# A listed order of work units, stores held back until the last load, and a narrower transpose stride in an attention and token-mixing kernel

## The chip, the cores and the metric

The kernel runs on one core of one Trainium2 chip. The metric is the device time of one execution in microseconds (us). A time is given as a median with the lowest and highest run. Runs more than 1.5% above the fastest run of the same kernel are counted as slow and take no part in ratios.

Engines are named as in the profile: PE is the tensor engine, PEld its weight loads, DVE the vector engine, ACT the scalar engine, POOL GpSimd, SP the sync engine that issues the stores.

## The reference

```python
# q, k, v: (8 batches, 8 heads, 576, 64) f32;  w_q, w_k: (512, 64);  w_out: (512, 512)
scores = scale * q_c @ k_c.T             # within chunks of 64 positions
attn   = softmax(scores)
x      = (attn @ v_c) as (8, 576, 512)   # heads side by side
wq, wk = x @ w_q, x @ w_k
W_tok  = scale * wq @ wk.T               # 576 x 576 for each batch
out    = relu(W_tok @ x) @ w_out         # (8, 576, 512) f32
```

## The kernel before

All of q, k and v is loaded by GpSimd, cast to f16 on the way, with one tile for each batch and part, so no load waits for a buffer. A batch is cut into units. T transposes q or k on DVE, in part 0 (5 row groups) or part 1 (4 row groups). S makes a quarter of the scores and their exponential. A multiplies them with v and divides. X transposes x on PE. K, Q and G are the small products of the mixing layer, M mixes, and O makes one of the 36 output tiles and stores it. Before the change a short list for one cycle is repeated, each unit with the lag that its inputs force, and four PSUM slots (places in the memory that matmuls write to) are taken in rotation:

```python
ORDER = "A3 M3 X0 O1 X1 Tk0 O1 K Tq0 Tq1 Q G S1 S0 O1 Tk1 M0 O1 O1 A0 S3 S2 A1 M1 M2 A2"

def pair(fill=0):                       # the next PSUM slot, in rotation
    turn[0] += 1
    a = ring[turn[0] % 4]
    for _ in range(fill):               # two 128x512 matmuls of zeros per unit of S, A, X in batch 0
        nc.tensor.matmul(a[:, 0, :], lhsT=zero[:, 0:P], rhs=zero[:], start=True, stop=True)
    return a

def tr(b, which):                       # q and k alike: f32 pairs written at stride 4 (16 bytes)
    nc.vector.transpose(out=dst[b % 2].bitcast(F32)[...].rearrange("p (t w r) -> p t r w", r=R, w=32), in_=...)

def outp():
    # ... four matmuls ...
    os_ = osb[n % NOSB]                 # five buffers
    nc.scalar.copy(os_[:], a[:, 0, :])
    nc.sync.dma_start(of[n * P : n * P + P, :], os_[:])   # the store goes at once
```

The loads are issued in this order: q and k of batch 0, its v, the weights, then batch after batch (cuts are marked by `...`).

The softmax here doesn't subtract the row's maximum and nothing guards it: scores larger than these inputs give would overflow.

Of the kernel before, what the change touches and what calls it, by code (L numbers as in the profile page):

```python
# [10 lines left out]
F16 = mybir.dt.float16  # L11
F32 = mybir.dt.float32
# [4 lines left out]
ORDER = """  # L17
A3 M3 X0 O1 X1 Tk0 O1 K Tq0 Tq1 Q G S1 S0 O1 Tk1 M0 O1 O1 A0 S3 S2 A1 M1 M2 A2
""".split()

NEEDS = {
    "S0": ("Tq0", "Tk0"),
    "S1": ("Tq0", "Tk0"),
    "S2": ("Tq1", "Tk1"),
    "S3": ("Tq1", "Tk1"),
    "A0": ("S0", "S1"),
    "A1": ("S0", "S1"),
    "A2": ("S0", "S1", "S2", "S3"),
    "A3": ("S2", "S3"),
    "X0": ("A0", "A1"),  # L30
    "X1": ("A2", "A3"),
    "Q": ("X0", "X1"),
    "K": ("X0", "X1"),
    "G": ("K", "X0", "X1"),
    "M0": ("Q", "G"),
    "M1": ("M0",),
    "M2": ("M1",),
    "M3": ("M2",),
}


def lags(order):
    at = {u: n for n, u in enumerate(order)}
    lag = {}

    def of(u):
        if u not in lag:
            lag[u] = max(
                [of(d) + (1 if at[d] > at[u] else 0) for d in NEEDS.get(u, ())] + [0]
            )  # L50
        return lag[u]

    for u in order:
        if u[0] != "O":
            of(u)
    return lag
# [3 lines left out]
def kernel(  # L60
# [32 lines left out]
    def each(n, shape, dt, name):  # L93
        return [sb.tile(shape, dt, name=f"{name}{i}") for i in range(n)]
# [21 lines left out]
    NOSB = 5  # L116
    osb = each(NOSB, [P, DM], F32, "osb")
# [15 lines left out]
    def load_v(b):  # L133
        nc.gpsimd.dma_start(  # L134
            vt[b][:, :, 0:D], vf[b].rearrange("(t p) d -> p t d", p=P)
        )

    nc.vector.memset(zero[:], 0.0)  # L138
    load_qk(0, 0)
    load_qk(0, 1)  # L140
    load_v(0)
    make_identity(nc, ident[:])
    nc.gpsimd.dma_start(wqd[:, :, 0:DH], moe_w_q.rearrange("(i p) j -> p i j", p=P))
    nc.gpsimd.dma_start(wk[:], moe_w_k.rearrange("(i p) j -> p i j", p=P))
    nc.gpsimd.dma_start(wout[:], moe_w_out.rearrange("(i p) m -> p i m", p=P))
    for b in range(1, B):
        load_qk(b, 0)
        load_v(b)
        load_qk(b, 1)
# [7 lines left out]
    turn = [0]  # L157

    def pair(fill=0):
        turn[0] += 1  # L160
        a = ring[turn[0] % 4]
        for _ in range(fill):
            nc.tensor.matmul(a[:, 0, :], lhsT=zero[:, 0:P], rhs=zero[:], start=True, stop=True)  # L163
        return a

    def tr(b, which):
        part = int(which[1])
        a, e = TR[part]
        src, dst = (qn, qT) if which[0] == "q" else (kn, kT)
        nc.vector.transpose(  # L170
            out=dst[b % 2]
            .bitcast(F32)[:, 2 * CH * a : 2 * CH * e]
            .rearrange("p (t w r) -> p t r w", r=R, w=32),
            in_=src[b][part].bitcast(F32).rearrange("p t (r d) -> p t r d", d=32),
        )

    def operand(buf, b, t, i, ch, e):
        o = t * R * D + ch * P
        return buf[b % 2][32 * i : 32 * i + 32, o : o + P].rearrange(
            "p (c e) -> p c e", e=2  # L180
        )[:, :, e]

    def scores(b, s, fill):
        rows, part = s % 2, s // 2
        t0, t1 = TR[part]
        a = pair(fill)
        for t in range(t0, t1):
            for e in range(2):
                for ch in range(2):
                    for i in range(2):  # L190
                        nc.tensor.matmul(  # L191
                            a[CH * ch : CH * ch + CH, i, (t - t0) * CH : (t - t0) * CH + CH],
                            lhsT=operand(kT, b, t, 2 * rows + i, ch, e),
                            rhs=operand(qT, b, t, 2 * rows + i, ch, e),
# [11 lines left out]
    def attend(b, kk, fill):  # L206
        a = pair(fill)
# [34 lines left out]
    def xtr(b, n, fill):  # L242
        a = pair(fill)
# [10 lines left out]
    def mlp_q(b):  # L254
        if b == 0:
            nc.vector.tensor_copy(wqd[:, :, DH:], wqd[:, :, 0:DH])  # L256
        a = pair()
# [11 lines left out]
    def mlp_k(b):  # L269
        a = pair()  # L270
# [13 lines left out]
    def mlp_g(b):  # L284
        a = pair()
# [11 lines left out]
    done = {"out": 0, "ready": 0}  # L297

    def mix(b, n):
        i, half = n % 2, n // 2  # L300
        a = pair()
# [15 lines left out]
        if i == 1:  # L317
            done["ready"] = ((2 * b + half + 1) * HS) // P

    def outp():  # L320
        n = done["out"]
        if n >= done["ready"]:
            return
        done["out"] = n + 1
        a = pair()
# [9 lines left out]
        os_ = osb[n % NOSB]  # L335
        nc.scalar.copy(os_[:], a[:, 0, :])  # L336
        nc.sync.dma_start(of[n * P : n * P + P, :], os_[:])

    lag = lags(ORDER)
    FILL = 2  # L340
    for _ in range(2):
        pair(7)
    for cycle in range(B + max(lag.values())):
        for u in ORDER:
            if u[0] == "O":
                outp()
                continue
            b = cycle - lag[u]
            if not 0 <= b < B:
                continue  # L350
            fill = FILL if b == 0 else 0
            if u[0] == "T":
                tr(b, u[1:])
            elif u[0] == "S":
                scores(b, int(u[1]), fill)
            elif u[0] == "A":
                attend(b, int(u[1]), fill)
            elif u[0] == "X":
                xtr(b, int(u[1]), fill)
            elif u == "Q":  # L360
                mlp_q(b)
            elif u == "K":
                mlp_k(b)
            elif u == "G":
                mlp_g(b)
            else:
                mix(b, int(u[1]))
    while done["out"] < done["ready"]:
        outp()
# [30 lines left out]
```

## Time and profile before

| | |
|---|---|
| time | 148.67 us median of the 3 runs (148.11 to 151.46) |
| span of the profiled execution | 149.3 us (one of the longer runs) |
| last load packet | 97.3 us |
| last matmul of the work | 145.4 us |
| data moved | 14.81 MB of loads as landed, 9.44 MB of stores |

The page, the batch windows and the four stalls are shown and read in the prediction below. First, windows cut where PE goes on past instructions 960 and 3008. Both numbers are 192 more than a multiple of 256, like those of the four stalls that the prediction shows in this trace (960, 1728, 2240 and 2752), each of which ended 2.3 to 2.5 us after the start of a packet of 16384 bytes on the queue that the page calls "instruction". The 256 instructions from one such place to the next are called a block here, and the place a boundary. The columns are: window, its length, then each engine's busy us with its instruction count, the granted clock of PE, DMA share, and GB/s.

```profile
core 0: us, PE busy (x) PEld busy (x) DVE busy (x) ACT busy (x) POOL busy (x), PEclk, DMA share, GB/s
0.00:39.85 39.85, 24.97 (x479) 12.74 (x479) 16.92 (x34) 7.33 (x11) 26.10 (x32) 0.76 1.61 165
39.85:96.99 57.14, 47.94 (x1023) 30.12 (x1024) 35.82 (x54) 27.84 (x48) 17.29 (x18) 0.81 1.70 210
96.99:149.30 52.31, 44.45 (x1001) 26.59 (x998) 30.79 (x46) 33.37 (x58) 0.00 (x0) 1.00 0.30 115
```

The middle row is eight blocks of 256 PE instructions (a matmul and a weight load count as two), 57.14 us. The q transposes among the groups of DVE: the last figure before the second bar is the mean length of one in ns.

```profile
L170 DVE STREAM_TRANSPOSE qT<-qn 128x640 f32<-128x640 f32 x8 | 10.4, 1295 | 0.0
...
L170 DVE STREAM_TRANSPOSE qT<-qn 128x512 f32<-128x512 f32 x8 | 8.6, 1072 | 0.0
```

### The profile page before, as it was taken

What the parts mean: (1) busy time and instruction counts of PE and PEld (TensorE: products, weight loads), DVE (VectorE), ACT (ScalarE), POOL (GpSimd) and SP (SyncE); (2) the same over time, 40 slices, a digit from 0 to 9 for tenths busy, and PEclk for the clock granted to TensorE, in tenths of its full rate; (3) what the DMA queues carried; (4) which work ended last, traced back from release to release, by engine and by line L of the source; (5) the groups of instructions that cost most, each with busy time, mean ns of one, the idle gap of its engine ahead of it and who ended that gap; (6) DMA issues with size and microseconds to landing.
All of it is one profiled execution on the core that took longest, in us unless ns stands there. A gap on an engine that the chain in (4) does not pass through costs nothing. (4 is left out here: it accounts for less than half of the span.)

```text
span 149.3 us, 5506 instructions
## 1 busy us (share of the span) xinstructions
PE 117.4 (79%) x2498; PEld 69.4 (47%) x2498; DVE 83.5 (56%) x133; ACT 68.5 (46%) x117; POOL 43.4 (29%) x49
## 2 busy tenths in 40 slices
PE   6626998176399881999689839989898798989890
PEld 2212436145166461564457426564574565566330
DVE  2082256932197764484577627493996799393000
ACT  3002200017143881139533836158748846864871
POOL 7996671662824612732730000000000000000000
PEclk9995557968659998579969995699999999999999
DMA  1999999999999999999999999921330312413254
GB/s 11 175 178 161 202 177 177 196 164 190 189 168 195 251 166 261 190 195 228 228 245 175 259 191 228 180 101 74 146 137 8 145 70 75 158 61 141 114 199 179
DMA packets 62725, 24.58 MB, mean 165 GB/s; under 512 B 39152, under 2 KB 58096, under 8 KB 62704
## 3 DMA queue, kind: packets, MB, share of 16 engines
q0 software_dynamic: 57520, 14.81, 100.5%
q1 hardware_dynamic: 5184, 9.44, 17.4%
q8 instruction: 19, 0.31, 0.8%
q14 instruction: 2, 0.02, 0.0%
HBM read 29.62 MB, written 9.44 MB: 262 GB/s over the span
## 5 line engine op out<-in xcount | busy, mean ns | idle before, releaser
L328 PE MATMUL ring<-wout,rmx 128*128 128x512 f16 x144 | 40.6, 416 | 0.4 <-ACT osb L336 0.2
L336 ACT COPY osb<-ring 128x512 f32<-128x512 f32 x36 | 21.1, 586 | 26.5 <-PE ring L328 25.8
L199 ACT ACTIVATE est<-ring 128x640 f16<-128x640 f32 (+1 forms) x32 | 19.6, 648 | 24.3 <-PE ring L191 23.9
L233 DVE TENSOR_TENSOR xn<-ring,rec 128x640 f16<-128x640 f32 x32 | 26.4, 824 | 1.1
L232 DVE RECIPROCAL rec<-ring 128x10 f32<-128x10 f32 x32 | 6.9, 217 | 32.7 <-PE ring L223 27.0
L191 PE MATMUL ring<-qT,kT 32*64 32x64 f16 x1152 | 14.7, 202 | 12.2 <-issue 5.8
L170 DVE STREAM_TRANSPOSE kT<-kn 128x640 f32<-128x640 f32 (+1 forms) x16 | 19.3, 1205 | 5.8 <-DMA kn<-in_k_dram 5.8
L311 ACT ACTIVATE rmx<-ring 128x576 f16<-128x576 f32 x32 | 19.8, 653 | 3.5 <-PE ring L303 3.1
L191 PEld LDWEIGHTS <-kT 32*64 32x64 f16 x1152 | 12.3, 111 | 17.8 <-issue 9.2
L328 PEld LDWEIGHTS <-rmx 128*128 128x128 f16 x144 | 13.5, 106 | 14.1 <-issue 3.6
L252 DVE COPY xt<-ring 128x1280 f16<-128x1280 f16 x16 | 13.2, 822 | 11.0 <-PE ring L247 10.7
L128 POOL DMA_DIRECT2D qn<-in_q_dram x16 | 13.1, 817 | 18.6 <-DMA vt<-in_v_dram 17.8
L247 PE MATMUL ring<-ident,xn 128*128 128x128 f16 x160 | 15.5, 258 | 3.5 <-issue 3.1
L170 DVE STREAM_TRANSPOSE qT<-qn 128x640 f32<-128x640 f32 (+1 forms) x16 | 17.7, 1184 | 0.0
L247 PEld LDWEIGHTS <-xn 128*128 128x128 f16 x160 | 13.1, 118 | 8.5 <-issue 6.8
L128 POOL DMA_DIRECT2D kn<-in_k_dram x16 | 13.0, 810 | 11.3 <-DMA kn<-in_k_dram 6.7
L134 POOL DMA_DIRECT2D vt<-in_v_dram x8 | 14.8, 1847 | 5.0 <-DMA kn<-in_k_dram 3.5
L223 PE MATMUL ring<-vt,est 64*64 64x65 f16 x576 | 12.4, 211 | 4.0 <-DVE xn L233 1.7
L223 PEld LDWEIGHTS <-est 64*64 64x64 f16 x576 | 9.1, 119 | 13.0 <-issue 9.9
L267 ACT CAST wqT<-ring 128x576 f16<-128x576 f32 x8 | 5.1, 638 | 21.7 <-PE ring L260 21.7
L163 PE MATMUL ring<-zero 128*128 128x512 f16 x34 | 13.9, 544 | 1.2 <-DVE zero L138 1.2
L260 PE MATMUL ring<-xt,wqd 128*128 128x288 f16 x64 | 9.9, 300 | 3.7 <-DVE wqd L256 3.7
(28 smaller groups left out, 69.8 us busy)
## 6 DMA issues: line engine op xcount, KB each, us to landing
out_dram<-osb SPq DMA_DIRECT2D x36, 256.0 KB, 2.5
vt<-in_v_dram POOLq DMA_DIRECT2D x8, 576.0 KB, 18.0
qn<-in_q_dram POOLq DMA_DIRECT2D x8, 320.0 KB, 14.2
kn<-in_k_dram POOLq DMA_DIRECT2D x8, 320.0 KB, 15.5
qn<-in_q_dram POOLq DMA_DIRECT2D x8, 256.0 KB, 17.6
kn<-in_k_dram POOLq DMA_DIRECT2D x8, 256.0 KB, 17.5
wout<-in_moe_w_out_dram POOLq DMA_DIRECT2D x1, 512.0 KB, 10.3
wqd<-in_moe_w_q_dram POOLq DMA_DIRECT2D x1, 64.0 KB, 8.0
```

Source lines behind the costliest of these rows:

```text
L128: nc.gpsimd.dma_start(dst[b][part][:], src[b].rearrange("(t p r) d -> p t (r d)", p=P, r=R)[:, a:e, :],)
L134: nc.gpsimd.dma_start(vt[b][:, :, 0:D], vf[b].rearrange("(t p) d -> p t d", p=P))
L163: nc.tensor.matmul(a[:, 0, :], lhsT=zero[:, 0:P], rhs=zero[:], start=True, stop=True)
L170: nc.vector.transpose(out=dst[b % 2] .bitcast(F32)[:, 2 * CH * a : 2 * CH * e] .rearrange("p (t w r) -> p t r w", r=R, w=32), in_=src[b][p ...
L191: nc.tensor.matmul(a[CH * ch : CH * ch + CH, i, (t - t0) * CH : (t - t0) * CH + CH], lhsT=operand(kT, b, t, 2 * rows + i, ch, e), rhs=oper ...
L199: nc.scalar.activation(est[b % 2][s].rearrange("p i t c -> p i (t c)")[:, :, 0:n], a[:, :, 0:n], AF.Exp, scale=scale_attn,)
L223: nc.tensor.matmul(a[CH * (c % 2) : CH * (c % 2) + CH, hh, jj * W : jj * W + D + 1], lhsT=lhsT, rhs=rhs, start=True, stop=True,)
L233: nc.vector.tensor_tensor(out=xn[b % 2][:, :, 2 * kk * D : 2 * kk * D + 2 * D].rearrange("p j (i d) -> p i j d", i=2), in0=xv[:, :, :, 0:D ...
L247: nc.tensor.transpose(tx[:, i, j * P : j * P + P], xn[b % 2][:, j, (2 * n + i) * P : (2 * n + i) * P + P], ident[:],)
L311: nc.scalar.activation(rmx[(b // 2) % 2].rearrange("p (h i) n -> p i h n", h=2)[:, i, :, o : o + HS], a[:, :, 0:HS], AF.Relu, scale=scale_moe,
L328: nc.tensor.matmul(a[:, 0, :], lhsT=rmx[pr % 2][:, i, tl * P : tl * P + P], rhs=wout[:, i, :], start=(i == 0), stop=(i == NI - 1),)
L336: nc.scalar.copy(os_[:], a[:, 0, :])
```

## The change

The change gives every unit its place by hand and takes the stores away from the loads. The whole program is one list of units with the PSUM slot after the colon (S31:0 is quarter 3 of the scores of batch 1, in slot 0). The idle fill matmuls are nearly gone. v of batch 0 comes in two halves, the first ahead of part 1 of q and k. The second half of wqd is loaded, not copied on DVE. q is transposed to stride 8 bytes, and the score matmuls read it accordingly. Each of the first 32 outputs lies in the q or k tile of a batch that is no longer needed, so no output waits for a buffer. A small copy out of the last loaded k tile stands ahead of the first store on the same queue, so that no store starts before the last load has landed (in the trace after, the last load packet ended at 88.3 us, and the sync engine issued the copy at 88.91 and the first store at 89.75); this copy is called the gate below. The diff is shortened: edits are left out without a mark, among them the function by which the score matmuls read q.

```diff
-ORDER = """ A3 M3 X0 O1 X1 Tk0 O1 K Tq0 Tq1 Q G S1 S0 O1 Tk1 M0 O1 O1 A0 S3 S2 A1 M1 M2 A2 """
+PLAN = """
+Tq00 Tk00 Tq10 S10:0 S00:1 Tk10 A00:2 S20:3 S30:0 A10:1 F:2 A20:2 A30:3 X00:0 X10:1 Tk01
+Tq01 Q0:2 K0:3 S11:0 S01:1 G0:2 A01:3 Tq11 M00:0 Tk11 A11:1 Tq02 M10:2 M20:0 Tk02 M30:3
+O:2 S31:0 S21:3 O:2 O:1 A21:0 A31:3 O:2 X01:1 S02:0 S12:2 X11:3 A02:0 K1:1 Tq12 Tk12
+... (ten more lines)
+"""
     load_qk(0, 0)
+    load_v(0, 0, NV // 2)
     load_qk(0, 1)
-    load_v(0)
+    load_v(0, NV // 2, NV)
-    nc.gpsimd.dma_start(wqd[:, :, 0:DH], moe_w_q.rearrange("(i p) j -> p i j", p=P))
+    nc.gpsimd.dma_start(wqd[:, :, 0:DH], wqv)
+    nc.gpsimd.dma_start(wqd[:, :, DH:], wqv)
+        if which[0] == "q":
+            o = o.rearrange("p (u w l) -> p u l w", l=2, w=32)
+        else:
+            o = o.rearrange("p (t w r) -> p t r w", r=R, w=32)
-        os_ = osb[n % NOSB]
-        nc.scalar.copy(os_[:], a[:, 0, :])
-        nc.sync.dma_start(of[n * P : n * P + P, :], os_[:])
+        if n < 4 * B:
+            home = (qn, kn)[n % 2][n // 4][(n // 2) % 2]
+            os_ = home.rearrange("p t c -> p (t c)").bitcast(F32)[:, 0:DM]
+        else:
+            os_ = spare[n - 4 * B][:]
+        nc.scalar.copy(os_, a[:, 0, :])
+        if n == GATE:                                    # GATE = 0
+            nc.sync.dma_start(mark[:], kn[B - 1][1][0:1, 0, 0:2])
+        nc.sync.dma_start(of[n * P : n * P + P, :], os_)
-    FILL = 2
... (the lags, the rotation and the per-unit fills are removed)
```

More of the change, by code (lines that the diff above doesn't have):

```diff
@@ L15 @@
 PSUM = bass.MemoryType.PSUM
-ORDER = """
-A3 M3 X0 O1 X1 Tk0 O1 K Tq0 Tq1 Q G S1 S0 O1 Tk1 M0 O1 O1 A0 S3 S2 A1 M1 M2 A2
-""".split()
-NEEDS = {
-    "S0": ("Tq0", "Tk0"),
-    "S1": ("Tq0", "Tk0"),
-    "S2": ("Tq1", "Tk1"),
-    "S3": ("Tq1", "Tk1"),
-    "A0": ("S0", "S1"),
-    "A1": ("S0", "S1"),
-    "A2": ("S0", "S1", "S2", "S3"),
-    "A3": ("S2", "S3"),
-    "X0": ("A0", "A1"),
-    "X1": ("A2", "A3"),
-    "Q": ("X0", "X1"),
-    "K": ("X0", "X1"),
-    "G": ("K", "X0", "X1"),
-    "M0": ("Q", "G"),
-    "M1": ("M0",),
-    "M2": ("M1",),
-    "M3": ("M2",),
-}
-def lags(order):
-    at = {u: n for n, u in enumerate(order)}
-    lag = {}
-    def of(u):
-        if u not in lag:
-            lag[u] = max(
-                [of(d) + (1 if at[d] > at[u] else 0) for d in NEEDS.get(u, ())] + [0]
-            )
-        return lag[u]
-    for u in order:
-        if u[0] != "O":
-            of(u)
-    return lag
+PLAN = """
+Tq00 Tk00 Tq10 S10:0 S00:1 Tk10 A00:2 S20:3 S30:0 A10:1 F:2 A20:2 A30:3 X00:0 X10:1 Tk01
+Tq01 Q0:2 K0:3 S11:0 S01:1 G0:2 A01:3 Tq11 M00:0 Tk11 A11:1 Tq02 M10:2 M20:0 Tk02 M30:3
+O:2 S31:0 S21:3 O:2 O:1 A21:0 A31:3 O:2 X01:1 S02:0 S12:2 X11:3 A02:0 K1:1 Tq12 Tk12
+Q1:2 G1:3 A12:0 Tq03 M01:1 M11:2 S22:3 Tk03 S32:1 X02:0 M21:2 O:3 S13:1 A22:2 S03:0
+A32:3 O:1 A03:2 M31:0 X12:3 Tq13 Tk13 A13:1 O:0 O:2 K2:3 Q2:0 S33:2 S23:1 Tq04 Tk04 G2:3
+O:0 A23:2 M02:1 M12:3 X03:0 A33:1 S04:2 S14:3 Tq14 O:0 X13:2 A04:1 M22:3 Tk14 O:0 Q3:2
+K3:3 M32:1 A14:0 S24:2 Tk05 S34:3 G3:1 O:0 A24:2 M03:3 Tq05 O:1 M13:0 A34:3 X04:2 S05:1
+S15:0 Tq15 X14:3 O:1 Tk15 O:2 K4:0 M23:3 A05:1 S25:2 Tq06 S35:0 G4:3 A15:1 M33:2 Q4:0
+A25:3 A35:2 X05:1 O:0 O:3 M04:2 M14:0 Tk06 O:1 X15:3 S06:2 S16:0 O:1 Tk16 Tq16 K5:3
+M24:2 A06:0 S36:1 S26:3 O:2 G5:0 M34:1 Tk07 A16:3 A26:2 Q5:0 Tq07 O:1 M05:3 A36:0 Tq17
+O:2 M15:1 Tk17 S17:3 S07:0 X16:2 X06:1 O:3 M25:2 A07:0 S27:1 K6:3 A17:2 S37:0 G6:1 M35:3
+A27:0 A37:2 Q6:1 O:3 M06:0 M16:1 X17:2 X07:3 O:0 O:2 K7:1 Q7:3 M26:0 M36:2 G7:1 O:3 O:0
+M07:2 M17:1 O:3 O:0 O:2 M27:1 M37:3 O:0 O:2 O:1 O:3 O:0
+"""
 @with_exitstack
@@ L115 @@
     rmx = each(2, [P, NI, 2 * S], F16, "rmx")
-    NOSB = 5
-    osb = each(NOSB, [P, DM], F32, "osb")
+    spare = each(4, [P, DM], F32, "spare")
+    mark = sb.tile([1, 2], F16, name="mark")
+    GATE = 0
     ring = [ps.tile([P, 2, 512], F32, name=f"ring{i}") for i in range(4)]
@@ L131, in load_qk, with load_v @@
             )
-    def load_v(b):
+    def load_v(b, lo, hi):
         nc.gpsimd.dma_start(
-            vt[b][:, :, 0:D], vf[b].rearrange("(t p) d -> p t d", p=P)
+            vt[b][:, lo:hi, 0:D],
+            vf[b].rearrange("(t p) d -> p t d", p=P)[:, lo:hi, :],
         )
@@ L139 @@
     load_qk(0, 0)
+    load_v(0, 0, NV // 2)
     load_qk(0, 1)
-    load_v(0)
+    load_v(0, NV // 2, NV)
     make_identity(nc, ident[:])
-    nc.gpsimd.dma_start(wqd[:, :, 0:DH], moe_w_q.rearrange("(i p) j -> p i j", p=P))
+    wqv = moe_w_q.rearrange("(i p) j -> p i j", p=P)
+    nc.gpsimd.dma_start(wqd[:, :, 0:DH], wqv)
+    nc.gpsimd.dma_start(wqd[:, :, DH:], wqv)
     nc.gpsimd.dma_start(wk[:], moe_w_k.rearrange("(i p) j -> p i j", p=P))
@@ L147 @@
         load_qk(b, 0)
-        load_v(b)
+        load_v(b, 0, NV)
         load_qk(b, 1)
@@ L155, with fill @@
     nc.vector.memset(padr[:, D:], 1.0)
-    turn = [0]
-    def pair(fill=0):
-        turn[0] += 1
-        a = ring[turn[0] % 4]
-        for _ in range(fill):
+    def fill(a, n):
+        for _ in range(n):
             nc.tensor.matmul(a[:, 0, :], lhsT=zero[:, 0:P], rhs=zero[:], start=True, stop=True)
-        return a
     def tr(b, which):
@@ L169, in tr, with k_of, q_of, scores @@
         src, dst = (qn, qT) if which[0] == "q" else (kn, kT)
+        o = dst[b % 2].bitcast(F32)[:, 2 * CH * a : 2 * CH * e]
+        if which[0] == "q":
+            o = o.rearrange("p (u w l) -> p u l w", l=2, w=32)
+        else:
+            o = o.rearrange("p (t w r) -> p t r w", r=R, w=32)
         nc.vector.transpose(
-            out=dst[b % 2]
-            .bitcast(F32)[:, 2 * CH * a : 2 * CH * e]
-            .rearrange("p (t w r) -> p t r w", r=R, w=32),
-            in_=src[b][part].bitcast(F32).rearrange("p t (r d) -> p t r d", d=32),
+            out=o, in_=src[b][part].bitcast(F32).rearrange("p t (r d) -> p t r d", d=32)
         )
-    def operand(buf, b, t, i, ch, e):
+    def k_of(b, t, i, ch, e):
         o = t * R * D + ch * P
-        return buf[b % 2][32 * i : 32 * i + 32, o : o + P].rearrange(
+        return kT[b % 2][32 * i : 32 * i + 32, o : o + P].rearrange(
             "p (c e) -> p c e", e=2
         )[:, :, e]
-    def scores(b, s, fill):
+    def q_of(b, t, i, ch, e):
+        o = t * R * D
+        return qT[b % 2][32 * i : 32 * i + 32, o : o + R * D].rearrange(
+            "p (h w l e) -> p w h l e", h=2, w=32, l=2
+        )[:, 16 * ch : 16 * ch + 16, :, :, e]
+    def scores(b, s, a):
         rows, part = s % 2, s // 2
         t0, t1 = TR[part]
-        a = pair(fill)
         for t in range(t0, t1):
@@ L192, in scores @@
                             a[CH * ch : CH * ch + CH, i, (t - t0) * CH : (t - t0) * CH + CH],
-                            lhsT=operand(kT, b, t, 2 * rows + i, ch, e),
-                            rhs=operand(qT, b, t, 2 * rows + i, ch, e),
+                            lhsT=k_of(b, t, 2 * rows + i, ch, e),
+                            rhs=q_of(b, t, 2 * rows + i, ch, e),
                             start=(e == 0),
@@ L204, in scores, with attend @@
         )
-    def attend(b, kk, fill):
-        a = pair(fill)
+    def attend(b, kk, a):
         for jj in range(NJ):
@@ L240, in attend, with xtr @@
         )
-    def xtr(b, n, fill):
-        a = pair(fill)
+    def xtr(b, n, a):
         tx = a.bitcast(F16)
@@ L252, in xtr, with mlp_q @@
         nc.vector.tensor_copy(xt[b % 2][n][:], tx[:, :, 0 : NJ * P])
-    def mlp_q(b):
-        if b == 0:
-            nc.vector.tensor_copy(wqd[:, :, DH:], wqd[:, :, 0:DH])
-        a = pair()
+    def mlp_q(b, a):
         for i in range(NI):
@@ L267, in mlp_q, with mlp_k @@
         nc.scalar.copy(wqT[b % 2].rearrange("p (h n) -> p h n", h=2), a[:, :, 0:HS])
-    def mlp_k(b):
-        a = pair()
+    def mlp_k(b, a):
         for j in range(NJ):
@@ L282, in mlp_k, with mlp_g @@
         )
-    def mlp_g(b):
-        a = pair()
+    def mlp_g(b, a):
         for j in range(NJ):
@@ L295, in mlp_g, with mix @@
         nc.scalar.copy(g16[b % 2][:], a[:, 0, 0 : DM // 2])
-    done = {"out": 0, "ready": 0}
-    def mix(b, n):
+    done = {"out": 0}
+    def mix(b, n, a):
         i, half = n % 2, n // 2
-        a = pair()
         for h in range(2):
@@ L316, in mix, with outp @@
         )
-        if i == 1:
-            done["ready"] = ((2 * b + half + 1) * HS) // P
-    def outp():
+    def outp(a):
         n = done["out"]
-        if n >= done["ready"]:
-            return
         done["out"] = n + 1
-        a = pair()
         pr, tl = n // NCH, n % NCH
@@ L334, in outp @@
             )
-        os_ = osb[n % NOSB]
-        nc.scalar.copy(os_[:], a[:, 0, :])
-        nc.sync.dma_start(of[n * P : n * P + P, :], os_[:])
-    lag = lags(ORDER)
-    FILL = 2
-    for _ in range(2):
-        pair(7)
-    for cycle in range(B + max(lag.values())):
-        for u in ORDER:
-            if u[0] == "O":
-                outp()
-                continue
-            b = cycle - lag[u]
-            if not 0 <= b < B:
-                continue
-            fill = FILL if b == 0 else 0
-            if u[0] == "T":
-                tr(b, u[1:])
-            elif u[0] == "S":
-                scores(b, int(u[1]), fill)
-            elif u[0] == "A":
-                attend(b, int(u[1]), fill)
-            elif u[0] == "X":
-                xtr(b, int(u[1]), fill)
-            elif u == "Q":
-                mlp_q(b)
-            elif u == "K":
-                mlp_k(b)
-            elif u == "G":
-                mlp_g(b)
-            else:
-                mix(b, int(u[1]))
-    while done["out"] < done["ready"]:
-        outp()
+        if n < 4 * B:
[7 more added lines that the diff above has]
+        nc.sync.dma_start(of[n * P : n * P + P, :], os_)
+    unit = {"S": scores, "A": attend, "X": xtr, "M": mix, "Q": mlp_q, "K": mlp_k, "G": mlp_g}
+    fill(ring[0], 7)
+    fill(ring[1], 7)
+    for u in PLAN.split():
+        u, _, slot = u.partition(":")
+        if u[0] == "T":
+            tr(int(u[3]), u[1:3])
+            continue
+        a = ring[int(slot)]
+        if u == "F":
+            fill(a, 1)
+        elif u == "O":
+            outp(a)
+        elif len(u) == 2:
+            unit[u[0]](int(u[1]), a)
+        else:
+            unit[u[0]](int(u[2]), int(u[1]), a)
 _INS = ['q', 'k', 'v', 'moe_w_q', 'moe_w_k', 'moe_w_out']
```

## The prediction

> **What bounds the kernel now.** I read the page first, then a table of windows cut at the k transposes that open each batch, then the tensor engine's timeline, its waits, and last the DMA packets of the trace. The profiled execution took 151.42 us (span 149.3); the median is 148.67, so this is one of the longer runs, and 2.1 us lie between span and time.
>
> ```profile
> PE 117.4 (79%) x2498; PEld 69.4 (47%) x2498; DVE 83.5 (56%) x133; ACT 68.5 (46%) x117; POOL 43.4 (29%) x49
> ...
> PEclk9995557968659998579969995699999999999999
> DMA  1999999999999999999999999921330312413254
> ...
> q8 instruction: 19, 0.31, 0.8%
> ```
>
> Loads fill the DMA engines for the first 26 slices, to 97 us (last packet 97.3). The granted clock dips only in that part. Queue 8 is the queue that fetches instructions: 19 packets, 0.31 MB, 0.8% of the engines' time. One row of windows is one batch:
>
> ```profile
> core 0: us, PE busy (x) PEld busy (x) DVE busy (x) ACT busy (x) POOL busy (x), PEclk, DMA share, GB/s
> 0.00:26.32 26.32, 19.08 (x280) 8.66 (x280) 11.13 (x26) 3.88 (x5) 18.20 (x25) 0.74 1.54 155
> 26.32:46.64 20.32, 12.44 (x298) 8.20 (x298) 10.33 (x18) 6.47 (x11) 10.31 (x11) 0.75 1.83 182
> 46.64:63.39 16.75, 12.70 (x306) 7.96 (x305) 10.39 (x17) 7.97 (x14) 8.41 (x9) 0.86 1.64 215
> 63.39:79.89 16.50, 14.79 (x315) 9.20 (x313) 10.37 (x16) 8.61 (x15) 6.46 (x7) 0.83 1.78 218
> 79.89:96.79 16.90, 13.70 (x307) 8.68 (x306) 10.32 (x17) 8.24 (x14) 0.00 (x0) 0.80 1.58 209
> 96.79:109.68 12.89, 11.80 (x313) 7.58 (x311) 10.12 (x17) 8.71 (x15) 0.00 (x0) 1.00 0.27 99
> 109.68:122.04 12.36, 11.10 (x309) 7.14 (x307) 10.19 (x16) 8.16 (x14) 0.00 (x0) 1.00 0.23 88
> ```
>
> The same batch takes 16.5 to 20 us under loads and 12.4 us after them. It does not wait for its data: the first k transpose is the only one that waits for a DMA. What costs the 4 to 8 us is seen on the tensor engine (PE):
>
> ```profile
> 39.85 0.26 PE L191 MATMUL ring<-qT,kT 32*64 32x64 f16 x3 [2.99 <-issue]
> ...
> 59.55 0.29 PE L247 MATMUL ring<-ident,xn 128*128 128x128 f16 x1 [3.11 <-issue]
> ...
> 73.79 0.42 PE L303 MATMUL ring<-wqT,g 64*128 64x288 f16 x3 [0.85 <-issue]
> ...
> 89.06 0.48 PE L191 MATMUL ring<-qT,kT 32*64 32x64 f16 x29 [2.52 <-issue]
> ```
>
> Four stalls in the middle of a unit, released by nothing. Counted in the trace, they stand at PE instructions 960, 1728, 2240 and 2752, each 192 more than a multiple of 256, and a packet of 16384 bytes on queue 8 starts 2.3 to 2.5 us before PE resumes (37.33, 57.25, 71.49, 86.62). Each such packet starts 2.4 to 4.3 us after PE passed the boundary before. So under loads a block of 256 PE instructions cannot follow the last in less than about 6.0 us (3.6 + 2.4). After the loads the packet starts 0 to 1.9 us after the boundary and nothing stalls so. Three of these stalls come with half clock (38.1 to 44.9, 58.6 to 65.4, 89.3 to 96.1 us), the short one by 3.4 us of it (75.7 to 79.1).
>
> [...] the 3.6 us under load are this trace's. [...] 1.30 us for a 640-column q transpose and 1.07 for 512, 2.0 to 2.1 ns per element.
>
> **The change part by part.**
> (1) The q transposes write at stride 8[...]. If that doubles the rate[...], 1.30 becomes 0.7 and 1.07 becomes 0.55: 8 x (0.6 + 0.5) = 9 us off DVE's 83.5, 1.1 per batch. DVE is busy 10.2 of 12.4 us per batch, PE 11.1, so little of it reaches the end; 0.3 per batch after the loads, counted in the waits of (5). The price: the matmuls of q read pairs 256 bytes apart. I assume no loss.
> (2) Twenty fill matmuls of 128x512 in batch 0 become one: about 10 us of PE in the first 24 us. v comes in halves and the first half before q and k of part 1, so batch 0's attention starts some 2 us sooner; the copy of wqd, on which PE waited 3.7 us, becomes a load of 64 KB (0.4 us at 180 GB/s). This removes the excess of the 26.32 and 20.32 us rows, but batch 1 cannot start before its data: the issue released by its last k part is at 28.96, so about 29.3 now, and with two transposes its second scores start at about 31.
> (3) Stores wait for the last load. By 45 us, with hardly a store, 7.39 of the 14.81 MB of loads had landed; the other 7.5 MB (with the second wqd) at 180 GB/s need 41.6 us: loads end at about 87, not 97.
> (4) The list holds 4960 PE rows. Instruction 960 falls in S31, at 31 us. From there to 87 the fetch admits 56 / 6.1 = 9.2 blocks: instruction 3300, where the kernel before stood at 2752. Pure work per block is only 3.0 to 5.8 us, so each block of this stage is fetch-bound; the order can't cure that.
> (5) What is left after instruction 3300, counted in the list, each unit at the distance from its start to the next one's in the timeline of the last window (full clock; O is one output tile, A attention, S scores, X the transposes of x, M mix): 21 O x 0.87 + 11 A x 0.30 + 4 S x 0.40 + 4 S x 0.33 + 6 X x 0.57 + 3 K x 0.75 + 4 Q x 1.08 + 4 G x 0.72 + 17 M x 0.24 = 41.4 us. A whole batch is 11.2 us by these figures and took 12.36, 10% more, in waits for the other engines. With the same 10% it is 45.6 us, and PE ends at 87 + 45.6 = 132.6. Before, the span ended 3.9 us after the last matmul (copy, store, end): 136.5, and with 2.1 the time is 138.6. The gated stores (18 of them, 4.7 MB) drain behind that work; the 9.44 MB took 17.4% of 149.3 us = 26 us of the 16 engines, so all fit well between 87 and 132. I predict 138.5.
>
> **The rivals.**
> (a) Half clock takes back the load stage. A stall of 1.5 us in each block may hold the clock down; a block of 4.4 us then takes about 7.5. 56 / 7.5 gives instruction 2870 at 87, 48.5 us of work left, and 53 + 87 + 6 = 146. For it: half clock after all four stalls. Against it: the gaps here are shorter and the long ones before were near 3 us.
> (b) Without stores the refill comes in 5 us; then PE's own 4.7 us per block binds, instruction 3776 is reached at 87, 31.7 us are left, and the time is 87 + 34.9 + 6 = 128. Against it: refills at 12 to 44 us, when no store ran, waited 2.8 to 4.1 us too.
> (c) The released stores become the new load: 18 at once and 4 more every 10 us may keep refills slow until 105. Three blocks at 6 instead of 4.7 us: +4, so 142.
> (d) q's matmuls slow down from the scattered read. S is 11.7 us of PE in all, and only the last 40% is not under the fetch: a third slower adds 1.5.
> (e) Nothing: if PE's order already hid all this, 148. Against it, the idle PE from 26 to 97 us.
>
> **Range and chances.** (a) and (c) pull up, (b) down; they leave 131.5 to 144.5 for 8 in 10. A gain under 2% (above 145.7) needs (a) in full: 6%. A loss needs something unseen, such as a vector queue blocked by a late load: 1%. Faster: 93%.
>
> **What would show it.** Stores absent until about 87 us and the last load packet there; q transposes of 0.7 and 0.55 us, k's unchanged; "issue" stalls on PE at nearly every 256 instructions before 87, none or few after; six to nine refills 6 us apart; batch rows near 12 us afterwards; PE past instruction 3000 at 87. Load end still near 97, or refills slow after 87, or half clock throughout would prove steps (3), (5) or (4) wrong.

## The result, and the profile after

| | before | after |
|---|---|---|
| time, us | 148.44 (148.11 to 151.46, 4 runs) | 137.38 (136.39 to 138.67, 4 runs) |
| ratio, 95% interval | 1 | 0.924 (0.914 to 0.934) |
| PE goes on past 960 | 39.85 | 31.82 |
| PE goes on past 3008 | 96.99 | 82.96 |
| last load packet | 97.3 | 88.3 |
| last matmul of the work | 145.4 | 132.8 |

A ratio, here and below, is the mean time of one kernel's fast runs over the mean of the other's fast runs of the same rounds, so it is not quite the ratio of the medians. Both profiled executions were among the slow ones of their sets (151.42 and 138.67 us).

First the page of the kernel after:

```profile
PE 108.6 (79%) x2479; PEld 66.8 (49%) x2479; DVE 78.3 (57%) x132; ACT 67.9 (50%) x117; POOL 44.8 (33%) x51
...
PEclk9995559559999595999599999959999999999999
DMA  0999999999999999999999999629999322242774
...
q8 instruction: 19, 0.31, 0.9%
```

A slice is now 136.6 / 40 = 3.4 us instead of 3.7. In the row of the DMA engines the loads end in the slice of the 6 (85.4 to 88.8 us), and the four 9s one slice later are the stores that had been held back. There are still 19 instruction packets. The clock is at full speed in more slices than before. The windows, cut at the same two instructions:

```profile
core 0: us, PE busy (x) PEld busy (x) DVE busy (x) ACT busy (x) POOL busy (x), PEclk, DMA share, GB/s
0.00:31.82 31.82, 20.60 (x478) 12.64 (x479) 16.89 (x36) 8.68 (x14) 23.60 (x30) 0.73 1.56 160
31.82:82.96 51.14, 40.47 (x1053) 25.46 (x1033) 33.26 (x53) 25.44 (x44) 21.17 (x22) 0.90 1.87 181
82.96:136.60 53.64, 47.52 (x977) 28.68 (x976) 28.16 (x45) 33.80 (x60) 0.00 (x0) 0.97 0.61 192
```

Set against the rows of the kernel before, 8.0 us are won up to instruction 960, 6.0 us in the eight blocks after it (6.4 us a block instead of 57.14 / 8 = 7.1), and 1.3 us are lost in the rest. Fast runs say the same of the block: 6.4 us in the control below, and 7.0 and 7.2 us in the two experiments that keep the old order and hold the stores back ("The gate alone", from 38.28 to 94.41 us, and "Start, gate and stride together"). The rest now starts 5 us before the load end, where it had started at it. The timeline of PE shows what sets the 6.4 us. Its columns are start, length, engine, line, operation, tiles and form, the number of instructions in the row, and in brackets the idle time before it with what ended it:

```profile
38.13 0.48 PE L173 MATMUL ring<-qT,kT 32*64 32x64 f16 x28 [1.54 <-issue]
...
44.87 0.79 PE L173 MATMUL ring<-qT,kT 32*64 32x64 f16 x56 [1.25 <-issue]
...
64.10 0.40 PE L277 MATMUL ring<-wqT,g 64*128 64x288 f16 x3 [1.67 <-issue]
...
76.77 0.31 PE L173 MATMUL ring<-qT,kT 32*64 32x64 f16 x11 [2.26 <-issue]
...
82.96 0.57 PE L173 MATMUL ring<-qT,kT 32*64 32x64 f16 x35 [1.05 <-issue]
...
89.16 0.56 PE L173 MATMUL ring<-qT,kT 32*64 32x64 f16 x31 [1.68 <-issue]
```

Counted in the trace (to within a few instructions), these stand at instructions 1216, 1472, 2240, 2752, 3008 and 3264. With those at 51.07 and 70.30, PE stalls at eight of the nine boundaries from 38 to 89 us, for 0.9 to 2.3 us. The profile names no releaser for any of them ("issue"), and each ended 2.3 to 2.6 us after a packet on the instruction queue had started. These packets of 16384 bytes start at 35.79, 42.32, 48.70, 55.30, 61.67, 67.94, 74.30, 80.51 and 86.87 us: (86.87 - 35.79) / 8 = 6.38 us apart. After the loads the page's clock is full again but for one dip, and the only stall of half a microsecond or more at a boundary is one of 0.56 us at 104.67. That is also seen in how soon a packet follows the moment at which PE goes on past a boundary: 3.7 to 4.2 us under the loads (as 42.32 after 38.13), 0.2 to 1.9 us from 95 to 107 us.

The sync engine's timeline shows the first store of an output:

```profile
89.75 0.67 SPq L312 DMA_DIRECT2D out_dram<-qn  x1
```

The loads had ended at 88.3. Twenty stores drained from 89.75 to 104.2 us. The q transposes:

```profile
L150 DVE STREAM_TRANSPOSE qT<-qn 128x640 f32<-128x640 f32 x8 | 6.7, 832 | 4.1 <-DMA qn<-in_q_dram 4.1
...
L150 DVE STREAM_TRANSPOSE qT<-qn 128x512 f32<-128x512 f32 x8 | 5.6, 703 | 2.0 <-DMA qn<-in_q_dram 2.0
```

They went from 1295 to 832 ns and from 1072 to 703 ns. The last column is their wait for the data of the first batch.

### The profile page after: what moved, and what is told of

It is laid out like the page before. It is cut to its first block, busy times and chain, and to the rows that moved or that the text cites. A ratio compares the mean times of both kernels' runs of the same rounds, so it can differ in the third digit from the quotient of the medians.

```text
span 136.6 us, 5492 instructions
## 1 busy us (share of the span) xinstructions
PE 108.6 (79%) x2479; PEld 66.8 (49%) x2479; DVE 78.3 (57%) x132; ACT 67.9 (50%) x117; POOL 44.8 (33%) x51
## 4 chain that ended last, share of the span: by engine, by line
PE 66%; issue 11%; DMA 8%; POOL 7%; DVE 4%; ACT 1%; DVEq 0%; POOLq 0%
PE ring L297 25%; PE ring L173 10%; DMA kn<-in_k_dram 8%; PE ring L227 7%; PE ring L237 6%; PE ring L204 6%; PE ring L277 5%; PE ring L263 5%; PE ring L249 3%; POOL qn L104 2%; POOL kn L104 1%; POOL vt L110 1%; DVE xt L232 1%; DVE kT L150 1%; DVE xn L214 1%
## 5 line engine op out<-in xcount | busy, mean ns | idle before, releaser
L297 PE MATMUL ring<-wout,rmx 128*128 128x512 f16 x144 | 38.5, 405 | 0.2
L173 PE MATMUL ring<-qT,kT 32*64 32x64 f16 x1152 | 16.2, 215 | 16.2 <-issue 7.8
L173 PEld LDWEIGHTS <-kT 32*64 32x64 f16 x1152 | 13.4, 114 | 20.1 <-issue 9.6
L110 POOL DMA_DIRECT2D vt<-in_v_dram x9 | 15.4, 1707 | 4.2 <-DMA kn<-in_k_dram 3.3
L150 DVE STREAM_TRANSPOSE qT<-qn 128x640 f32<-128x640 f32 (+1 forms) x16 | 12.3, 767 | 6.0 <-DMA qn<-in_q_dram 6.0
L227 PE MATMUL ring<-ident,xn 128*128 128x128 f16 x160 | 13.3, 243 | 0.0
L309 ACT COPY kn<-ring 128x512 f32<-128x512 f32 x16 | 9.4, 589 | 7.6 <-PE ring L297 7.4
L309 ACT COPY qn<-ring 128x512 f32<-128x512 f32 x16 | 9.4, 588 | 7.4 <-PE ring L297 5.9
L227 PEld LDWEIGHTS <-xn 128*128 128x128 f16 x160 | 11.2, 111 | 2.1 <-issue 1.3
L237 PE MATMUL ring<-xt,wqd 128*128 128x288 f16 x64 | 10.7, 316 | 0.0
```

The source lines that it names most:

```text
L110: nc.gpsimd.dma_start(vt[b][:, lo:hi, 0:D], vf[b].rearrange("(t p) d -> p t d", p=P)[:, lo:hi, :],)
L150: nc.vector.transpose(out=o, in_=src[b][part].bitcast(F32).rearrange("p t (r d) -> p t r d", d=32))
L173: nc.tensor.matmul(a[CH * ch : CH * ch + CH, i, (t - t0) * CH : (t - t0) * CH + CH], lhsT=k_of(b, t, 2 * rows + i, ch, e), rhs=q_of(b, t, ...
L227: nc.tensor.transpose(tx[:, i, j * P : j * P + P], xn[b % 2][:, j, (2 * n + i) * P : (2 * n + i) * P + P], ident[:],)
L237: nc.tensor.matmul(a[:, h, 0:HS], lhsT=wqd[:, i, :], rhs=xt[b % 2][i // 2][:, i % 2, h * HS : h * HS + HS], start=(i == 0), stop=(i == NI ...
L297: nc.tensor.matmul(a[:, 0, :], lhsT=rmx[pr % 2][:, i, tl * P : tl * P + P], rhs=wout[:, i, :], start=(i == 0), stop=(i == NI - 1),)
```

## The experiments

The theory: under loads PE is limited by the fetch of its own instructions, one block in about 6.4 us, and the change wins by reaching this stage earlier, by ending it earlier, and by making its blocks even. The rivals: the gain is PE's or DVE's lighter work (fills, transposes); the stage is bound by PE's work or by the data; any traffic on the DMA engines slows the fetch. The experiments ran on two chips, where the kernel before took 149.8 to 150.5 us; every ratio is to the runs of the kernel before on the same chip.

### The kernel after once more

No edit: the control for all others, in five rounds.

> The changed kernel itself, as the control for the runs beside it on this chip: ratio to the kernel before 0.915 to 0.934 again. Stalls at every block boundary until about 88 us and none after, as in its first profile.

Measured: 137.04 us (136.70 to 137.32, 6 runs), ratio 0.916 (0.912 to 0.921). PE goes on past 3008 at 82.96 as in the first trace, and ends at 131.5. This is the figure that the parts below are set against. It is a fast run, and its eight blocks take (82.96 - 31.94) / 8 = 6.4 us, too:

```profile
31.94:82.96 51.02, 40.01 (x1052) 24.94 (x1033) 33.14 (x53) 25.43 (x44) 21.09 (x22) 0.91 1.87 181
```

### No gate

The copy ahead of the first store is taken out; outputs still lie in the dead tiles.

```diff
         nc.scalar.copy(os_, a[:, 0, :])
-        if n == GATE:
-            nc.sync.dma_start(mark[:], kn[B - 1][1][0:1, 0, 0:2])
         nc.sync.dma_start(of[n * P : n * P + P, :], os_)
```

> The changed kernel without the gate: stores go out as soon as their copy is done. Fetch theory: the stores delay the loads, which end at 96 to 97 us instead of 88; instruction blocks stay 6.3 to 6.5 us apart until then, so about 1.3 more blocks run at 6.4 instead of 4.9 us: 2 us more, 139.5 us. Rival, that the gate is the main gain: 144 or more.

Measured: 139.13 us (138.81 to 139.41), ratio 0.928 (0.925 to 0.931), so within the list the gate is worth about 1.2% (0.928 against 0.916). The loads ended at 99.8 us instead of 88.3, yet PE went on past 3008 at 82.72 and its last matmul ended at 132.9, as in the first trace of the kernel after. Eleven more microseconds of loads cost so little because only two blocks of PE fell into them. The first, to instruction 3520 at 95.82, took 6.90 us, partly at half clock, against 6.95 in the first trace of the kernel after and 5.55 in the control; the next took 4.72 us in all three. The only long stall for instructions after 89 us was one of 0.95 us at 104.77.

### The old stride for q

The q transposes and the q operand of the score matmuls are as before, all else as after.

```diff
-        if which[0] == "q":
-            o = o.rearrange("p (u w l) -> p u l w", l=2, w=32)
-        else:
-            o = o.rearrange("p (t w r) -> p t r w", r=R, w=32)
+        o = o.rearrange("p (t w r) -> p t r w", r=R, w=32)
```

> The changed kernel with the q transposes of the kernel before (stride 16) and its q operand. Theory: transposes are back at 1.30 and 1.07 us, 7 us more of VectorE, mostly under the fetch stalls: 0.5 to 1.5 us more, 138 to 139. The score matmuls, at 215 ns mean now and 202 before, may give part of it back. Rival, VectorE on the path: 4 us or more.

Measured: 137.64 us (137.02 to 138.53), ratio 0.918 (0.913 to 0.924), which is not distinguishable from the control. The transposes were back at 1322 and 1090 ns, so 0.4 to 0.5 us each was given up, and no time was lost that can be measured. DVE is not on the path that sets the end. The score matmuls' mean went from 215 to 204 ns: the scattered read costs PE 11 ns in each. The 1152 of them overlap (1152 x 215 ns = 248 us of records in 16.2 us of busy time), so the busy time went only from 16.2 to 14.9 us, and that shows in no time either.

### The start alone

The kernel before with no fills, v of batch 0 in halves, and the second half of wqd loaded.

```diff
+    load_v(0, 0, NV // 2)
     load_qk(0, 1)
-    load_v(0)
+    load_v(0, NV // 2, NV)
+    nc.gpsimd.dma_start(wqd[:, :, DH:], wqv)
-        if b == 0:
-            nc.vector.tensor_copy(wqd[:, :, DH:], wqd[:, :, 0:DH])
-    FILL = 2
+    FILL = 0
```

> The kernel before with three edits alone: no fill matmuls in batch 0, v of batch 0 in two halves with the first ahead of q and k of part 1, the second half of wqd loaded and not copied. Theory: instruction 960 is reached at about 33 instead of 39.9 us, and the time falls by 4 to 6 us to about 143.5. Rival, that the fetch-bound stage absorbs it (it waits later for loads): under 2 us.

Measured: 147.38 us (146.52 to 148.15), ratio 0.983 (0.977 to 0.989): 2.5 us, less than expected. The trace shows that the start itself did all it should: PE went on past 960 at 31.83 instead of 39.85. But from there to its last matmul at 141.2 it took 109.4 us, where the kernel before took 105.5 (in a slow run, and with 40 more instructions left, as its first 960 hold the 20 fills; so if anything the loss is larger). Its outputs, and so its stores, came earlier and fell among the loads, which ended at 101.6 us, later than the 97.3 of before, and PE still waited for instructions then:

```profile
100.67 0.42 PE L305 MATMUL ring<-wqT,g 64*128 64x288 f16 x1 [2.79 <-issue]
```

The clock was at half from 99.7 to 106.5 us with it. Of the 8.0 us won at the start, 3.9 were given back later.

### The gate alone

The kernel before with the outputs in dead tiles and the stores held back.

```diff
-        os_ = osb[n % NOSB]
-        nc.scalar.copy(os_[:], a[:, 0, :])
+        if n < 4 * B:
+            home = (qn, kn)[n % 2][n // 4][(n // 2) % 2]
+            os_ = home.rearrange("p t c -> p (t c)").bitcast(F32)[:, 0:DM]
+        else:
+            os_ = spare[n - 4 * B][:]
+        nc.scalar.copy(os_, a[:, 0, :])
+        if n == GATE:
+            nc.sync.dma_start(mark[:], kn[B - 1][1][0:1, 0, 0:2])
```

> The kernel before with the gate and the outputs in dead tiles alone. Loads end at 87 to 88 us, not 97; the old order keeps its dense and light blocks. Theory: 9 us less of load stage spares one long stall and its half clock, 4 us of 148.4 (ratio 0.965 to 0.98). Rival, that the gate is worth as little as in the list, where taking it away cost about half a per cent: 0.99 to 1.0.

Measured: 148.49, 151.06, 150.85 and 151.03 us beside a kernel before of 149.99 (148.46 to 151.50). Three of the four runs are over 1.5% above the fastest, so no ratio is given; the medians differ by 0.6%. No gain is shown, and the expectation of 2 to 3.5% failed. The loads did end at 88.2 us. The profile happened to be the fastest run, and the last matmul in it ended at 142.6. Why three runs took 151 us stays open.

### Start, gate and stride together, in the old order

The two edits above and the stride of 8 bytes in one kernel, with the old list and its rotation of slots. The diff is the sum of the two above and the change's own edit of the transpose.

> Everything of the change but the list: the old rotating order and the old slots in turn, with the new start, the gate with the outputs in dead tiles, and stride 8. Theory: start 5, gate 2, stride 1 off 148.4 gives about 141; the rest, 3 us, is the list, which spreads the instruction-dense units so that no block waits long (blocks 7.1 us apart in the old order, 6.3 in the list). Rival, that the list is the main gain: 144 or more; that it is nothing: 138.

Measured: 142.49 us (140.69 to 143.35), ratio 0.946 (0.939 to 0.954), as expected. Alone the start gave 1.7% and the gate no gain that shows; together, with the stride, they give 5.4%. Here PE went on past 960 at 31.33, the loads ended at 88.1, and the last long stall was at 81.59 instead of the 100.67 of the start alone. What the start wins is kept better when the stores are out of the loads. (That the stride adds nothing is shown with the new list only, not in this order.)

The rest, from 0.946 to 0.916, is 3.2%, or 4 to 5 us: the list with its slots and the single fill. It lies in the load stage. The same eight blocks, 960 to 3008, in this kernel (the cut at 31.06 is 0.3 us early):

```profile
31.06:88.96 57.90, 48.59 (x1041) 31.27 (x1031) 34.24 (x54) 28.50 (x50) 21.81 (x23) 0.79 1.79 174
```

and in the kernel after 51.14 us, with 40.47 us of PE busy at a clock of 0.90. (These are more than the 4 to 5 us because the kernel after, when it reaches 3008, still has 5 us of loads before it, and this kernel has none.) The number of matmuls is the same to about 1%. The clock is not. In the traces before and after, the clock granted inside the span is either full or half (0.50 from 45.10 to 48.40 us in the one after, 1.00 from 48.50 to 51.80); if it is so here, too, 0.79 means 2 x 0.21 x 57.90 = 24 us at half clock, and 0.90 means 2 x 0.10 x 51.14 = 10 us. With the old order PE goes on past the boundaries at 31.33, 40.97, 47.68, 55.55, 60.89, 67.37, 75.72, 81.59 and 88.96: blocks of 5.3 to 9.6 us. Light blocks end in stalls of 2.94, 3.13 and 2.17 us, each followed by 3.4 to 6.9 us of half clock, in which the next, heavy block is then slow. With the list the blocks take 6.2 to 6.8 us. That evenness is the cause is read from the two traces; the slots were not tried apart from the order.

### Batches 3 to 7 not loaded

The result is wrong: their tiles are set to a constant by GpSimd, and the gate waits for batch 2.

```diff
-    for b in range(1, B):
+    for b in range(1, 3):
         load_qk(b, 0)
         load_v(b, 0, NV)
         load_qk(b, 1)
+    for b in range(3, B):
+        for x in (*qn[b], *kn[b]):
+            nc.gpsimd.memset(x[:], 0.1)
+        nc.gpsimd.memset(vt[b][:, :, 0:D], 0.1)
-            nc.sync.dma_start(mark[:], kn[B - 1][1][0:1, 0, 0:2])
+            nc.sync.dma_start(mark[:], kn[2][1][0:1, 0, 0:2])
```

> Wrong result on purpose: batches 3 to 7 are not loaded, their tiles are set by GpSimd; all else of the changed kernel stays, the gate waits for batch 2. Fetch theory: from about 39 us no PE stall at block boundaries is left, a block takes about 4.9 us, and the time falls to 127 to 129. Rival, that PE's own work or its clock sets the pace before 88 us: 136 to 137.

Measured in one round: 122.02 us (121.24 and 122.80), ratio 0.813. That is 5 us more gain than expected. The page and one window:

```profile
PEclk9997555955899999999999999999999999999999
DMA  0999999999998360342222224024223220324782
```

```profile
38.00:100.00 62.00, 61.12 (x1758) 40.88 (x1759) 54.39 (x87) 42.42 (x75) 15.71 (x13) 1.00 0.28 101
```

Once the loads are gone, PE is busy 61.12 of 62.00 us at full clock. A block then takes (91.66 - 43.41) / 11 = 4.39 us instead of 6.38, and no long stall at a boundary comes after 38.11 us. Stores still run. So it is the loads that hold PE, and not through data: in the kernel after no transpose of q or k waited for a load after 33 us (the last such wait, 0.28 us, ended at 32.25).

### Half the score matmuls

Wrong: only the even half of the depth is summed, 1152 of PE's 4958 instructions fewer, all loads kept. (The check of the result does not see this fault.) If data or a fixed period per batch bound the load stage, PE's share of batches would not move; if the fetch of blocks does, a batch with fewer instructions passes sooner.

```diff
-            for e in range(2):
+            for e in range(1):
-                            start=(e == 0),
-                            stop=(e == 1),
+                            start=True,
+                            stop=True,
```

> Wrong result on purpose: the score matmuls of the odd halves are left out, 576 matmuls and as many weight loads, 1152 of 4960 PE instructions, and 5 to 6 us of PE's work. Theory, the instruction fetch paces the load stage: a batch is 1.9 instead of 2.4 blocks, the list stands about a batch further at 88 us, and the time falls by 9 to 13 us to 125 to 128. Rival, PE's work sets the pace: 5 to 6 us off, 131 to 132.

Measured: 123.39 us (122.56 to 123.97), ratio 0.825 (0.819 to 0.831), slightly more than the theory gave and clearly not the rival's value. PE still stalls in the load stage:

```profile
50.06 0.38 PE L297 MATMUL ring<-wout,rmx 128*128 128x512 f16 x1 [0.65 <-issue]
...
56.81 0.19 PE L204 MATMUL ring<-padr,padl 64*64 64x65 f16 x1 [1.16 <-issue]
...
63.28 0.19 PE L204 MATMUL ring<-padr,padl 64*64 64x65 f16 x1 [0.75 <-issue]
```

These and the next two (69.47, 76.49) are on average (76.49 - 50.06) / 4 = 6.6 us apart and stand at instructions 1472, 1728, 1984, 2240 and 2496 of the shorter program. They meet other units than in the kernel after, because 256 instructions reach further into a batch. The period belongs to the block of instructions and not to the batch.

### More loads after the last, on GpSimd's queue

Twenty half-v loads, f32 cast to f16, follow the last real one into four scratch tiles that nothing reads.

```diff
+    again = each(4, [P, NV // 2, D], F16, "again")
+    for n in range(20):
+        nc.gpsimd.dma_start(
+            again[n % 4][:],
+            vf[n % B].rearrange("(t p) d -> p t d", p=P)[:, 0 : NV // 2, :],
+        )
```

> The changed kernel with 20 more loads of half a v tile each by the same GpSimd queue, into scratch that nothing reads, after the last real load; the gate does not wait for them. Fetch theory: the stage with refills 6.3 us apart goes on to about 110 us; four blocks that took 5.0 us take 6.3: 5 us more, 142. Rival, that the stalls have to do with the program's place and not with the loads: 137.4 to 138.

Measured: 157.09 us (156.83 to 157.29), ratio 1.047. The time is not the test that was meant: the extra loads lasted to 153.7 us, and they set the end. The last matmul is the test: it ended at 146.3 us instead of 132.8, though no instruction of PE depends on these loads. Stalls go on where the kernel after has none:

```profile
97.56 0.38 PE L303 MATMUL ring<-wout,rmx 128*128 128x512 f16 x1 [1.33 <-issue]
...
104.03 0.31 PE L210 MATMUL ring<-vt,est 64*64 64x65 f16 x14 [1.38 <-issue]
...
110.50 0.32 PE L210 MATMUL ring<-vt,est 64*64 64x65 f16 x6 [3.19 <-issue]
```

The instruction packets start at 88.32, 95.27, 101.75, 108.27, 114.79, 122.02 and 128.67 us, 6.7 us apart on average, and some 4.2 us after PE goes on past a boundary (101.75 after 97.56, 108.27 after 104.03), as under the real loads. This is the load stage made longer, and nothing else was changed.

### The same reads from the sync engine

Twenty reads of the same DRAM areas, without a cast, are issued by the sync engine, one after each of the first 20 stores.

```diff
+    again = each(2, [P, NV // 2, D], F32, "again")
         nc.sync.dma_start(of[n * P : n * P + P, :], os_)
+        if n < 20:
+            nc.sync.dma_start(
+                again[n % 2][:],
+                vf[n % B].rearrange("(t p) d -> p t d", p=P)[:, 0 : NV // 2, :],
+            )
```

> The same bytes read from DRAM (20 halves of v), but issued by the sync queue, without the cast, one after each store. If any full DMA engine delays a refill: as with the loads of the GpSimd queue, about 142. If it is the packets of the software queue that refills wait behind: refills stay within 2 us of their boundary, and the time stays within 1 us of 137.4.

Measured: 172.04 us (171.49 to 172.35), ratio 1.146. Again the transfers themselves set the end, which neither theory had allowed for, so the time decides nothing. PE does: its last matmul ended at 133.9 us, 1.1 us later than in the first trace of the kernel after (132.8) and 2.4 later than in the control's (131.5), where the loads on GpSimd's queue had moved it by 13.5 or more. The window from 88 to 134 us, first with the extra loads on GpSimd's queue, then with those from the sync engine:

```profile
88.00:134.00 46.00, 35.02 (x819) 21.57 (x818) 25.50 (x41) 21.65 (x38) 15.95 (x14) 0.89 1.88 229
```

```profile
88.00:134.00 46.00, 42.75 (x904) 25.57 (x902) 26.06 (x42) 31.40 (x58) 0.00 (x0) 1.00 1.05 235
```

At nearly the same GB/s PE did 904 matmuls instead of 819, at full clock. After 90 us the instruction packets started 0.7 to 3.0 us after PE went on past a boundary, where it had been 4.2 us with GpSimd's loads and 0.2 to 1.9 with stores alone. Part of this is longer than the 2 us that the second theory allowed, and two stalls at boundaries were long, 1.20 us at 104.16 and 1.40 at 114.64. So equal traffic delays the fetch far less when it is not on GpSimd's queue. The two also differ in packet sizes, in the cast, and in the time that the packets occupy the engines (1.88 against 1.05 in the column before the last), and which of these matters was not tried.

### The weights of the output moved behind batch 1

The load of wout stands after the loads of batch 1, so that batch 1 comes sooner.

```diff
-    nc.gpsimd.dma_start(wout[:], moe_w_out.rearrange("(i p) m -> p i m", p=P))
     for b in range(1, B):
         ...
+        if b == 1:
+            nc.gpsimd.dma_start(wout[:], moe_w_out.rearrange("(i p) m -> p i m", p=P))
```

> The changed kernel with the load of the output weights (512 KB) moved behind batch 1's loads. If the start waits for batch 1's q and k (VectorE waits 2.8 us for k until 22.8 us), instruction 960 is reached 2 to 2.8 us sooner, and the time falls by about 2 us to 135.4, below both kernels. Rival, that the next wait takes it over (the refill of block 960, or the first output that now waits for its weights): no change.

Measured: 137.67 us (137.15 to 137.90), ratio 0.917 (0.910 to 0.923), the same as the control. The wait had only moved:

```profile
29.01 1.89 PE L298 MATMUL ring<-wout,rmx 128*128 128x512 f16 x4 [3.10 <-DMA wout<-in_moe_w_out_dram]
```

The first output tile now waited 3.10 us for wout, and PE went on past 960 at 31.3, 0.6 us sooner than the control (31.9).

### The same, with the first output tiles later in the list

To use the earlier batch 1, the first four O units are moved back among the S and A of batch 1 and the slots of these units are chosen anew.

```diff
-O:2 S31:0 S21:3 O:2 O:1 A21:0 A31:3 O:2 X01:1 S02:0 S12:2 X11:3 A02:0 K1:1 Tq12 Tk12
-Q1:2 G1:3 A12:0 ...
+S31:0 S21:2 O:3 O:1 A21:0 O:3 A31:2 O:1 X01:3 S02:0 S12:2 X11:1 A02:0 K1:3 Tq12 Tk12
+Q1:2 G1:1 A12:0 ...
```

> Late load of the output weights, and in the list the first two scores of batch 1's part 1 stand ahead of the first outputs, which then no longer hold them up (a wait of 3.1 us until 29.0 us with the late load alone). Theory: instruction 960 is passed at 29.0 to 29.5, when its block lands, not at 31.3 to 31.8; the fetch-bound stage keeps this lead, and the time falls by 1.5 to 2.5 us below the changed kernel (ratio to it 0.982 to 0.99). Rival: batch 2's data or a refill takes it over before 45 us, and nothing is left.

Measured: 138.15 us (136.38 to 138.54), ratio 0.921 (0.914 to 0.927), against 0.916 for the control: no gain. PE went on past 960 at 29.07, nearly 3 us sooner. At instruction 3264 the lead was down to 89.16 - 87.93 = 1.2 us, and the stall there was longer:

```profile
87.93 0.53 PE L174 MATMUL ring<-qT,kT 32*64 32x64 f16 x31 [2.23 <-issue]
```

Half clock followed from 88.5 to 91.9, and PE reached 3520 at 94.98, where the control reached it at 94.71. The lead was gone. Part of that is chance: the stall of 1.68 us at this place brought half clock in the first trace of the kernel after and none in the control's. The medians of six runs show no gain all the same. So no kernel of these beats the one after the change.

## Why the prediction was right or wrong

Its time, 138.5 us, was right to about 1 us, and so was its mechanism: a load stage bound by the fetch of PE's instructions (6.38 us a block, and 4.39 where the loads were gone).

- **Steps (2) and (4), the entry.** Instruction 960 was put at 31 us; PE went on past it at 31.82. As a step it was right, but the start alone is worth 1.7%, not the whole lead: 3.9 of 8.0 us were lost again later, while the loads lasted longer.
- **Step (3), the end of the loads.** Predicted 87, measured 88.3. As a separate gain it was not found: the gate alone showed none, and in the list it is worth 1.2%. Its worth depends on what else is in the loads.
- **Step (4), the block.** Predicted 6.1 us, measured 6.38. It put PE at instruction 3300 at 87 us; PE reached 3264 at 87.27, so it sized the sum well. (The list has 4958 PE instructions, not 4960.) That "a block of 256 PE instructions cannot follow the last in less than about 6.0 us" is not true of single blocks: its own trace has one of 4.55 us under the loads (48.52 to 53.08), after one of 8.66. What keeps its distance is the packets, which start 6.25 to 8.8 us apart there from 37 us on. The sentence "the order can't cure that" is the one that failed. It is true of the 6.4 us floor; it is false of the stage, of which it also said that each block is fetch-bound, because the kernel before took 7.1 us a block and the old order with every other edit took 57.90 / 8 = 7.2. The list removed this excess. The prediction took the floor for the period, and did not ask why the kernel before, above the same floor, took 7.1.
- **Step (5), the rest.** Predicted 45.6 us from 87 on; from 87.27 to the last matmul at 132.8 it was 45.5, and about 44.2 in the control's fast run. The sum held, but not for its reason alone: 1.68 us of it were one more stall for instructions at 3264, and in the first trace 3.4 us after it ran at half clock, neither of which is a wait for another engine.
- **Step (1), the transposes.** Predicted 0.7 and 0.55 us, on the assumption that the narrower stride doubles the rate; measured 0.83 and 0.70. The rate did about double: (832 - 703) / 128 = 1.0 ns for each further element against (1295 - 1072) / 128 = 1.7. What the step left out is a fixed part of about 832 - 640 x 1.0 = 192 ns. No time came of it, as the old stride's run shows.
- **Rival (a), half clock**, went the other way: stalls of 0.9 to 2.3 us in nearly every block came with fewer dips (0.90 against 0.81). The length of a gap alone does not tell whether a dip follows: half clock came from 45.03 to 48.44 us, after the stall of 1.25 us that ended at 44.87, and none came with the one of 2.26 us that ended at 76.77. **Rival (b)**, a faster fetch without stores, did not happen: 6.38 us a block without them, and the kernel without the gate passed 3008 at the same time. (Its working also slips: with a refill of 5 us the refill and not PE's 4.7 us would bind, and 3776 is what 5.1 us a block gives.) **Rival (c)**, a burst of stores that slows the fetch: 319 GB/s were moved from 90 to 105 us, nearly all of it stores, and the instruction packets then started only 0.2 to 1.9 us after PE went on past a boundary. **Rival (d)**, slower q matmuls: 215 against 204 ns, no time.

Two things stay open: what in GpSimd's queue makes the fetch wait (the run from the sync engine shows only that equal GB/s from there delay it far less), and how much of the list's gain is order and how much its choice of PSUM slots.

## What to carry to other kernels

When an engine stalls with nothing to release it, count its instructions. Here the stalls stood multiples of 256 apart, each ended 2.2 to 2.6 us after a packet on the instruction queue had started, and with the loads of batches 3 to 7 taken away no long one came after 38.11 us: they are read as the engine's wait for its own instructions. What counted then was how many instructions lay under the loads and, as far as two traces tell, how evenly the work was spread over the blocks, not which engine was busy. Test a part of a change with the others in place as well as alone; here two parts gave 1.7% and no gain that shows when alone, and 5.4% together with a third that was worth nothing in the list. A faster operation on an engine that nothing waits for, or a lead that runs into a later wait, was worth nothing here, and one experiment each settled it.
